# A cached-attention decode step with a gated MLP: output projections in column layout, the group tail deferred, eight K blocks prefetched

## The chip, the cores and the metric

The kernel runs on one core of a Trainium2 chip. The metric is device time in microseconds (us) of a whole execution; shorter is better. Six runs of the kernel before took between 417.31 and 419.82 us, with a median of 418.4 us.

## What is computed

One token goes through two branches whose results are mixed by a scalar gate. Branch A is attention with 32 query heads, 4 key/value heads and a cache of 65,536 positions. Branch B is a gated MLP on the same token. All tensors are bf16.

```
x = A_x                                        # (1, 1, 1024)
g = sigmoid((x * gate_w).sum(-1))
q = x @ wq                                     # 32 heads of 128
s = q @ k_cache^T * 128**-0.5                  # 4 KV heads, 8 query heads each, 65536 positions
a = (softmax(s) @ v_cache) @ wo                # wo: (4096, 1024)
z = gelu(x @ w_in)                             # w_in: (1024, 3584)
u = z[:1792] * (w_sp * layernorm(z[1792:]) + b_sp)
b = u @ w_out                                  # w_out: (1792, 1024)
out = g * a + (1 - g) * b                      # (1, 1, 1024)
```

K and V are 64 MiB each, the weights 26.5 MiB together; every byte is read once.

## The kernel before, in words

The kernel works in four **groups**, one for each KV head g. The cache of a group is cut into 16 K blocks and 16 V blocks of 4,096 positions (1 MiB each). Every large tile (K and V blocks, and all weight tiles) comes from one pool of 19 buffers of 8 KB per partition (`kv`, L83, `NKV = 19`), and all of these loads are issued on the queue of SP, in the order in which the program emits them. A scheduler in the framework settles the order on every engine, gives out buffers, and makes a load wait until its buffer is free. Each load also waits for the completion of the load eight places earlier, because there are eight semaphores for transfers; so eight are in flight at most.

**K blocks** (`k_block_work`, L290): a block has 32 chunks of 128 positions. PE transposes each chunk (`tps`, L296), eight to a PSUM tile; VectorE (DVE) or ScalarE (ACT) copies the tile to SBUF (`ktt`, L301 and L303); PE multiplies it with the eight query heads of the group (`spt`, L263). For every 64 chunks ACT casts the scores to `scT` (L271) and DVE takes a maximum over them (`mxp`, L275).

**stats** (L324), once per group after its last K block: the maximum over all positions goes through a transpose (`mxT`) and a matmul with ones (`nb_ps`) to `negm` on all partitions.

**The V phase**: in five parts, DVE adds `negm` to the scores (L444), ACT takes Exp (L448), DVE sums up (`Ssum`, L450), and PE accumulates 512 matmuls per group into one PSUM tile, `o_ps` (L456), 32 for each V block. There is one buffer for `o_ps`. Between V blocks the loop slips in other loads with their work: the two `wo` tiles of the group (`woa_t`), a few tiles of `w_in` with their `z` matmuls (L176), and the first `XK` K blocks of the next group. In the last group it slips in the four tiles of `w_out` (`wout_t`) instead.

**group_tail** (L342) ends each group: `l_ps` and its reciprocal, scaling of `o_ps` (`o_sc`, L351), a transpose to `oT` (L354, L355), and the product with this group's rows of `wo` (L365). Here the vector oT is the stationary operand (128 x 1) and `wo` the moving one (128 x 512), so that the result is one row of 1,024 on one partition, in two halves. DVE adds them to `a_acc` (L372, L374). `b_matmuls` (L237) makes `b_row` in the same way from `uT` and `w_out`. After the tail, the remaining K blocks of the next group follow, with the first `XV` = 3 V blocks among them.

**The end** (L479 to L484): two DVE instructions on one partition, `diff` and `orow`, mix a_acc, b_row and the gate, and one transfer writes the row. The gate itself is made at the start on one partition too, from `x_row` and `gw_row` (L113 to L118).

The loop over groups, before, in the lines that matter:

```
for g in range(G):
    flush_k(g)
    negm = stats(g)
    ...
    group_tail(g, o_ps, Ssum)
    if not last:
        rem = list(range(XK, NBLK))
        ...
```

Of the kernel before, what the change touches and what calls it, by code (L numbers as in the profile page):

```python
# [20 lines left out]
PST_BUFS = 3  # L21
LAG = 3
XV = 3
XK = 4


@with_exitstack
def kernel(
# [49 lines left out]
    win_groups = [min(i * (G - 1) // NWIN, G - 2) for i in range(NWIN)]  # L78

    const = ctx.enter_context(tc.tile_pool(name="const", bufs=1))  # L80
    rows = ctx.enter_context(tc.tile_pool(name="rows", bufs=1))
    wk = ctx.enter_context(tc.tile_pool(name="wk", bufs=2))
    kv = ctx.enter_context(tc.tile_pool(name="kv", bufs=NKV))  # L83
    ktp = ctx.enter_context(tc.tile_pool(name="ktp", bufs=KT_BUFS))
# [12 lines left out]

    x8 = const.tile([KC, P], BF16, name="x8")
    nc.scalar.dma_start(out=x8[:], in_=A_x.rearrange("o t (kc p) -> (o t kc) p", p=P))
    x_row = rows.tile([1, D], BF16, name="x_row")  # L100
    nc.scalar.dma_start(out=x_row[:], in_=A_x.rearrange("o t d -> (o t) d"))
    gw_row = rows.tile([1, D], BF16, name="gw_row")
    nc.scalar.dma_start(out=gw_row[:], in_=gate_w.rearrange("(o d) -> o d", o=1))
    wsp_b = const.tile([P, 1], BF16, name="wsp_b")
    nc.scalar.dma_start(out=wsp_b[:], in_=B_w_sp.rearrange("a b -> (a b)").to_broadcast((P, 1)))
    bsp_b = const.tile([P, 1], BF16, name="bsp_b")
# [3 lines left out]
    bsp_f = const.tile([P, 1], FP32, name="bsp_f")  # L110
    nc.vector.tensor_copy(out=bsp_f[:], in_=bsp_b[:])

    gprod = rows.tile([1, D], FP32, name="gprod")  # L113
    nc.vector.tensor_tensor(out=gprod[:], in0=x_row[:], in1=gw_row[:], op=ALU.mult)
    gsum = wk.tile([1, 1], FP32, name="gsum")
    nc.vector.reduce_sum(out=gsum[:], in_=gprod[:], axis=AX.X)
    gate = const.tile([1, 1], FP32, name="gate")
    nc.scalar.activation(out=gate[:], in_=gsum[:], func=ACT.Sigmoid)  # L118

    xT_ps = psm.tile([P, KC], BF16, name="xT_ps", tag="m")  # L120
    nc.tensor.transpose(xT_ps[:], x8[:], ident_b[:KC, :KC])  # L121
    xT = const.tile([P, KC], BF16, name="xT")
    nc.vector.tensor_copy(out=xT[:], in_=xT_ps[:])

    qacc = const.tile([P, H], FP32, name="qacc")
    for kc in range(KC):
# [96 lines left out]
                                scalar2=bsp_f[:, 0:1], op0=ALU.mult, op1=ALU.add)  # L223
        nc.vector.tensor_tensor(out=uT[:], in0=zg[:, 0:KC_OUT], in1=gb[:], op=ALU.mult)

    b_row = rows.tile([1, D], FP32, name="b_row")

    def b_matmuls():
        b_ps = [psm.tile([1, 512], FP32, name=f"b_ps{nb}", tag="m") for nb in range(NBH)]
        for i in range(NWOUT):  # L230
            ch0 = i * WO_CH
            ncks = min(WO_CH, KC_OUT - ch0)
            wo_t = wout_tiles[i]
            for kl in range(ncks):
                kcg = ch0 + kl
                for nb in range(NBH):
                    nc.tensor.matmul(  # L237
                        b_ps[nb][:, :], lhsT=uT[:, kcg:kcg + 1],
                        rhs=wo_t[:, kl, nb * 512:(nb + 1) * 512],
                        start=(kcg == 0), stop=(kcg == KC_OUT - 1),  # L240
                    )
        for nb in range(NBH):
            nc.vector.tensor_copy(out=b_row[:, nb * 512:(nb + 1) * 512], in_=b_ps[nb][:, :])  # L243

    oT = const.tile([P, H], BF16, name="oT")
    a_acc = rows.tile([1, D], FP32, name="a_acc")
    evac_i = [0]
    gs = [SimpleNamespace(scT=None, mxp=None, pending=[], spt=None, v_tiles={}) for _ in range(G)]

# [74 lines left out]
    def stats(g):  # L324
        st = gs[g]
        mx = wk.tile([P, REP], FP32, name="mx")
        nc.vector.tensor_reduce(out=mx[:], in_=st.mxp[:].rearrange("p b h -> p h b"),  # L327
                                axis=AX.X, op=ALU.max)
        mxT = psm.tile([REP, P], FP32, name="mxT", tag="m")
        nc.tensor.transpose(mxT[:], mx[:], ident_f[:])  # L330
        gm = wk.tile([REP, 1], FP32, name="gm")
        nc.vector.reduce_max(out=gm[:], in_=mxT[:], axis=AX.X)
        dg = wk.tile([REP, REP], FP32, name="dg")
        nc.vector.tensor_scalar(out=dg[:], in0=ident_f[:REP, :REP], scalar1=gm[:, 0:1],
                                scalar2=-1.0, op0=ALU.mult, op1=ALU.mult)
        nb_ps = psm.tile([P, REP], FP32, name="nb_ps", tag="m")
        nc.tensor.matmul(nb_ps[:], lhsT=ones_f[:REP, :], rhs=dg[:], start=True, stop=True)  # L337
        negm = wk.tile([P, REP], BF16, name="negm")
        nc.vector.tensor_copy(out=negm[:], in_=nb_ps[:])
        return negm  # L340

    def group_tail(g, o_ps, Ssum):  # L342
        ssum = wk.tile([P, REP], FP32, name="ssum")
        nc.vector.tensor_reduce(out=ssum[:], in_=Ssum[:].rearrange("p b h -> p h b"),
                                axis=AX.X, op=ALU.add)
        l_ps = psm.tile([REP, 1], FP32, name="l_ps", tag="m")
        nc.tensor.matmul(l_ps[:], lhsT=ssum[:], rhs=ones_f[:, 0:1], start=True, stop=True)
        rl = wk.tile([REP, 1], FP32, name="rl")
        nc.vector.reciprocal(out=rl[:], in_=l_ps[:])
        o_sc = wk.tile([REP, DH], BF16, name="o_sc")  # L350
        nc.vector.tensor_scalar(out=o_sc[:], in0=o_ps[:], scalar1=rl[:, 0:1], scalar2=None,  # L351
                                op0=ALU.mult)
        oT_ps = psm.tile([P, REP], BF16, name="oT_ps", tag="m")
        nc.tensor.transpose(oT_ps[:], o_sc[:], ident_b[:REP, :REP])  # L354
        nc.vector.tensor_copy(out=oT[:, g * REP:(g + 1) * REP], in_=oT_ps[:])  # L355
        a_ps = [psm.tile([1, 512], FP32, name=f"a_ps{nb}", tag="m") for nb in range(NBH)]
        for gi in range(WOA_PER_G):
            wi = g * WOA_PER_G + gi
            h0 = wi * WOA_CH
            woa = woa_tiles[wi]  # L360
            for hl in range(WOA_CH):
                h = h0 + hl
                hl_g = gi * WOA_CH + hl
                for nb in range(NBH):
                    nc.tensor.matmul(  # L365
                        a_ps[nb][:, :], lhsT=oT[:, h:h + 1],
                        rhs=woa[:, hl, nb * 512:(nb + 1) * 512],
                        start=(hl_g == 0), stop=(hl_g == REP - 1),
                    )
        for nb in range(NBH):  # L370
            if g == 0:
                nc.vector.tensor_copy(out=a_acc[:, nb * 512:(nb + 1) * 512], in_=a_ps[nb][:, :])  # L372
            else:
                nc.vector.tensor_tensor(out=a_acc[:, nb * 512:(nb + 1) * 512],  # L374
                                        in0=a_acc[:, nb * 512:(nb + 1) * 512],
                                        in1=a_ps[nb][:, :], op=ALU.add)

    def spread_positions(n, lo, hi):
        if n == 0:
# [7 lines left out]
    for blk in range(NBLK):  # L387
        kn = k_block_dma(0, blk)
        k_block_work(0, blk, kn)
        if blk in vpos0:  # L390
            v_block_dma(0, vb_next)
            vb_next += 1

    for g in range(G):
        flush_k(g)
        negm = stats(g)

        last = (g == G - 1)
        if not last:
# [63 lines left out]
            c0 += ceb  # L463
        assert not callbacks, callbacks.keys()

        group_tail(g, o_ps, Ssum)

        if not last:
            rem = list(range(XK, NBLK))
# [2 lines left out]
            for ri, blk in enumerate(rem):  # L472
                kn = k_block_dma(g + 1, blk)
                k_block_work(g + 1, blk, kn)
                if ri in vpos:
                    v_block_dma(g + 1, vb_next)
                    vb_next += 1

    diff = rows.tile([1, D], FP32, name="diff")  # L479
    nc.vector.tensor_tensor(out=diff[:], in0=a_acc[:], in1=b_row[:], op=ALU.subtract)  # L480
    orow = rows.tile([1, D], BF16, name="orow")
    nc.vector.scalar_tensor_tensor(out=orow[:], in0=diff[:], scalar=gate[:, 0:1], in1=b_row[:],
                                   op0=ALU.mult, op1=ALU.add)
    nc.sync.dma_start(out=out.rearrange("o t d -> (o t) d"), in_=orow[:])  # L484


# [28 lines left out]
```

## Time and profile before

| | |
|---|---|
| Median of six runs | 418.4 us |
| Profiled execution: whole time | 417.55 us |
| Profiled execution: span from the first instruction to the last | 415.8 us |
| PE (matmul) busy | 349.2 us (84%), 6,743 instructions |
| PE weight loads busy | 321.6 us (77%) |
| DVE busy | 209.3 us (50%), 325 instructions |
| ACT busy | 126.9 us (31%), 145 instructions |
| Read from HBM | 162.01 MB, 390 GB/s over the span |
| Granted clock of PE, mean | 0.963 |

The span is what the page and its views divide; the whole time has 1.75 us more around it. PE's matmuls are pipelined: one record of a matmul lasts longer than the distance to the next, so that a cost is taken from a row of many, as duration over count. The page's slices show the busy share of each engine in forty equal parts of the span (10.4 us each), in tenths; the row PEclk shows the clock that PE was granted, DMA the mean busy share of the sixteen DMA engines, and GB/s what they moved. A group takes about 92 us: four stretches of K work, stats and V work follow each other. The timeline has instructions in order of time: start, duration, engine, line, operation, result and operands, shapes and count, and in brackets how long the engine had been idle and what ended that.

### The profile page before, as it was taken

The numbers are of one execution on the slowest core, as the hardware profiler recorded it, in microseconds if no ns is written. First come the engines' busy times: TensorE is split into PE (matmuls) and PEld (weight loads), VectorE is DVE, ScalarE is ACT, GpSimd is POOL, SyncE is SP. The second block draws the span as 40 slices with busy tenths as digits, with TensorE's granted clock in tenths as the row PEclk, the third lists the DMA queues.
The fourth block names the chain that finished last, engine by engine and source line by source line (L and its number), as shares of the span: only waits on it lengthen the run. The fifth ranks groups of instructions, "written<-read, shape, count | busy, mean of one in ns | idle before, by whom it ended". The sixth has DMA issues, their size and how long they took to land.

```text
span 415.8 us, 14558 instructions
## 1 busy us (share of the span) xinstructions
PE 349.2 (84%) x6743; PEld 321.6 (77%) x6743; DVE 209.3 (50%) x325; ACT 126.9 (31%) x145; POOL 0.8 (0%) x7
## 2 busy tenths in 40 slices
PE   0548899789989999779999988859999998869993
PEld 0548888779988788779997777759999688868781
DVE  1224677792243486682142666675443576783014
ACT  1004454640031354431122444442231254550000
POOL 0000000000000000000000000000000000000000
PEclk9999999969999999969999999969999999969998
DMA  7999999999999999999999999999999999999930
GB/s 269 424 415 418 420 413 415 403 415 417 415 417 418 419 415 412 404 418 418 415 418 418 417 418 412 403 416 419 419 414 419 420 411 411 391 412 401 372 128 0
DMA packets 27186, 162.94 MB, mean 392 GB/s; under 512 B 2803, under 2 KB 2803, under 8 KB 9718
## 3 DMA queue, kind: packets, MB, share of 16 engines
q1 hardware_dynamic: 26818, 162.02, 95.4%
q8 instruction: 52, 0.85, 0.8%
q10 hardware_dynamic: 308, 0.01, 0.0%
q14 instruction: 8, 0.07, 0.0%
HBM read 162.01 MB, written 0.00 MB: 390 GB/s over the span
## 4 chain that ended last, share of the span: by engine, by line
PE 64%; ACT 13%; DVE 10%; DMA 6%; issue 6%; ACTq 1%; DVEq 0%
PE o_ps L456 30%; PE tps L296 19%; ACT ktt L301 10%; PE spt L263 7%; DVE ktt L303 6%; DMA kn<-in_A_k_cache_dram 4%; DMA bsp_b<-in_B_b_sp_dram 3%; ACT scT L271 2%; PE z_ps L176 2%; DVE mxp L275 1%; PE b_ps_8170 L237 1%; PE b_ps_8171 L237 1%; PE nb_ps L337 1%; PE a_ps_8245 L365 0%; PE a_ps_4644 L365 0%
## 5 line engine op out<-in xcount | busy, mean ns | idle before, releaser
L296 PE MATMUL tps<-ident_b,kn 128*128 128x128 bf16 x2048 | 138.4, 222 | 13.4 <-DVE ktt L303 7.8
L303 DVE COPY ktt<-tps 128x1024 bf16<-128x1024 bf16 x171 | 112.4, 686 | 70.4 <-PE tps L296 67.7
L301 ACT COPY ktt<-tps 128x1024 bf16<-128x1024 bf16 x85 | 86.0, 1012 | 181.9 <-PE tps L296 181.9
L296 PEld LDWEIGHTS <-kn 128*128 128x128 bf16 x2048 | 120.5, 99 | 19.0 <-issue 16.5
L456 PE MATMUL o_ps<-vt,scT 128*8 128x128 bf16 x2048 | 127.0, 226 | 4.1 <-ACT scT L448 4.1
L456 PEld LDWEIGHTS <-scT 128*8 128x8 bf16 x2048 | 121.5, 90 | 5.7 <-ACT scT L448 4.5
L263 PE MATMUL spt<-qT,ktt 128*128 128x8 bf16 x2048 | 76.8, 167 | 9.7 <-ACT ktt L301 4.5
L263 PEld LDWEIGHTS <-ktt 128*128 128x128 bf16 x2048 | 67.1, 96 | 15.2 <-ACT ktt L301 8.0
L275 DVE TENSOR_REDUCE mxp<-scT 128x8 f32<-128x512 bf16 x32 | 34.0, 1061 | 29.8 <-ACT scT L271 29.7
L450 DVE TENSOR_REDUCE Ssum<-scT 128x8 f32<-128x1024 bf16 (+2 forms) x20 | 31.0, 1596 | 2.4 <-ACT scT L448 2.4
L271 ACT CAST scT<-spt 128x512 bf16<-128x512 f32 x32 | 18.8, 588 | 19.0 <-PE spt L263 19.0
L448 ACT ACTIVATE scT<-scT 128x1024 bf16<-128x1024 bf16 (+2 forms) x20 | 16.7, 879 | 21.3 <-DVE scT L444 21.1
L131 PEld LDWEIGHTS <-wq_t 128*128 128x128 bf16 x256 | 7.2, 104 | 17.2 <-issue 13.0
L121 PE MATMUL xT_ps<-ident_b,x_94 8*128 8x8 bf16 x1 | 0.2, 161 | 15.0 <-DVE ident_b L94 15.0
L365 PEld LDWEIGHTS <-oT 128*1 128x1 bf16 x64 | 5.0, 84 | 8.7 <-DVE oT L355 1.4
L243 DVE COPY b_row<-b_ps_8170 1x512 f32<-1x512 f32 x1 | 0.7, 679 | 21.2 <-PE b_ps_8170 L237 21.2
L131 PE MATMUL q_ps<-xT,wq_t 128*128 128x1 bf16 x256 | 7.4, 165 | 4.3 <-DMA wq_t<-in_A_wq_dram 4.0
L183 DVE TENSOR_TENSOR zacc<-zacc,z_ps 128x28 f32<-128x28 f32 x7 | 1.3, 183 | 19.2 <-PE z_ps L176 19.2
L444 DVE TENSOR_TENSOR scT<-scT,negm 128x1024 bf16<-128x1024 bf16 (+2 forms) x20 | 10.6, 578 | 0.1
L330 PE MATMUL mxT<-ident_f,mx 128*8 128x128 f32 x4 | 1.4, 348 | 8.3 <-DVE mx L327 8.3
L351 DVE TENSOR_SCALAR o_sc<-o_ps,rl 8x128 bf16<-8x128 f32 x4 | 1.4, 339 | 12.8 <-PE o_ps L456 12.8
L330 PEld LDWEIGHTS mxT<-ident_f,mx 128*8 128x8 f32 x4 | 0.3, 83 | 8.7 <-DVE mx L327 6.5
(79 smaller groups left out, 87.2 us busy)
## 6 DMA issues: line engine op xcount, KB each, us to landing
kn<-in_A_k_cache_dram SPq DMA_DIRECT2D x64, 1024.0 KB, 19.9
vt<-in_A_v_cache_dram SPq DMA_DIRECT2D x64, 1024.0 KB, 19.9
wq_t<-in_A_wq_dram SPq DMA_DIRECT2D x8, 1024.0 KB, 10.6
woa_t<-in_A_wo_dram SPq DMA_DIRECT2D x8, 1024.0 KB, 20.1
wi_t<-in_B_w_in_dram SPq DMA_DIRECT2D x8, 896.0 KB, 18.5
wout_t<-in_B_w_out_dram SPq DMA_DIRECT2D x3, 1024.0 KB, 19.0
wout_t<-in_B_w_out_dram SPq DMA_DIRECT2D x1, 512.0 KB, 18.2
x_94<-in_A_x_dram ACTq DMA_DIRECT2D x1, 2.0 KB
```

Of the source, the lines that this page charges most:

```text
L131: nc.tensor.matmul(q_ps[:, h:h + 1], lhsT=wq_t[:, h * DH:(h + 1) * DH], rhs=xT[:, kc:kc + 1], start=True, stop=True,)
L176: nc.tensor.matmul(z_ps[:, mc:mc + 1], lhsT=wi_t[:, mc * P:(mc + 1) * P], rhs=xT[:, kc:kc + 1], start=True, stop=True,)
L263: nc.tensor.matmul(spt[:, (cg % CPS) * REP:(cg % CPS + 1) * REP], lhsT=lhs_getter(j), rhs=qT[:, g * REP:(g + 1) * REP], start=True, stop=True,
L271: nc.scalar.copy(out=st.scT[:, cb * CPS:(cb + 1) * CPS, :], in_=spt[:, :].rearrange("p (c h) -> p c h", h=REP),)
L275: nc.vector.tensor_reduce(out=st.mxp[:, cb, :], in_=st.scT[:, cb * CPS:(cb + 1) * CPS, :].rearrange("p c h -> p h c"), axis=AX.X, op=ALU.max,)
L296: nc.tensor.transpose(tps[:, j * P:(j + 1) * P], kn[:, c0 + j, :], ident_b[:])
L301: nc.scalar.copy(out=ktt[:], in_=tps[:])
L303: nc.vector.tensor_copy(out=ktt[:], in_=tps[:])
L444: nc.vector.tensor_tensor(out=scT[:, c0:c0 + ceb, :], in0=scT[:, c0:c0 + ceb, :], in1=negm[:].unsqueeze(1).to_broadcast([P, ceb, REP]), op ...
L448: nc.scalar.activation(out=PT[:, c0:c0 + ceb, :], in_=scT[:, c0:c0 + ceb, :], func=ACT.Exp, scale=SCALE)
L450: nc.vector.tensor_reduce(out=Ssum[:, eb, :], in_=PT[:, c0:c0 + ceb, :].rearrange("p c h -> p h c"), axis=AX.X, op=ALU.add,)
L456: nc.tensor.matmul(o_ps[:, :], lhsT=PT[:, cg, :], rhs=st.v_tiles[blk][:, c, :], start=(cg == 0), stop=(cg == NCG - 1),)
```

## The change

Five edits:

- **Column layout.** In `group_tail` and `b_matmuls` the weights are now the stationary operand (128 x 128) and the vector the moving one (128 x 1). The result is a tile of 128 partitions x 8 columns; column `nch` holds outputs 128 nch to 128 nch + 127. 16 matmuls of N = 512 per group become 64 of N = 1, and 28 become 112. The loop over output chunks is now the outer one, so that each column is accumulated to its end before the next begins. `a_acc`, `bT`, the differences and the mix are 128 x 8.
- **Output.** The 128 x 8 result is transposed on PE to 8 x 128 and written as eight rows.
- **Gate.** x and `gate_w` are loaded as 8 x 128, transposed, multiplied, summed per partition, and added up over partitions by a matmul with ones. The two row tiles and their pool go.
- **Deferred tail.** The tail of groups 0 to 2 is called after the `stats` of the next group; that of group 3 stays where it was.
- **XK = 8** in place of 4: eight K blocks of the next group come in the V phase, eight after it.

```diff
-XK = 4
+XK = 8
...
     def b_matmuls():
-        b_ps = [psm.tile([1, 512], FP32, name=f"b_ps{nb}", tag="m") for nb in range(NBH)]
...
+        b_ps = psm.tile([P, NCH_O], FP32, name="b_ps", tag="m")
+        for nch in range(NCH_O):
+            for kcg in range(KC_OUT):
+                i, kl = divmod(kcg, WO_CH)
+                wo_t = wout_tiles[i]
+                nc.tensor.matmul(
+                    b_ps[:, nch:nch + 1],
+                    lhsT=wo_t[:, kl, nch * P:(nch + 1) * P],
+                    rhs=uT[:, kcg:kcg + 1],
+                    start=(kcg == 0), stop=(kcg == KC_OUT - 1),
+                )
+        nc.vector.tensor_copy(out=bT[:], in_=b_ps[:])
...
+        a_ps = psm.tile([P, NCH_O], FP32, name="a_ps", tag="m")
+        for nch in range(NCH_O):
+            hl_g = 0
+            for gi in range(WOA_PER_G):
...
                     nc.tensor.matmul(
-                        a_ps[nb][:, :], lhsT=oT[:, h:h + 1],
-                        rhs=woa[:, hl, nb * 512:(nb + 1) * 512],
+                        a_ps[:, nch:nch + 1],
+                        lhsT=woa[:, hl, nch * P:(nch + 1) * P],
+                        rhs=oT[:, h:h + 1],
                         start=(hl_g == 0), stop=(hl_g == REP - 1),
                     )
...
+    deferred_tail = None
     for g in range(G):
         flush_k(g)
         negm = stats(g)
+        if deferred_tail is not None:
+            group_tail(*deferred_tail)
+            deferred_tail = None
...
-        group_tail(g, o_ps, Ssum)
+        if not last:
+            deferred_tail = (g, o_ps, Ssum)
+        else:
+            group_tail(g, o_ps, Ssum)
...
-    nc.vector.tensor_tensor(out=diff[:], in0=a_acc[:], in1=b_row[:], op=ALU.subtract)
...
-    nc.sync.dma_start(out=out.rearrange("o t d -> (o t) d"), in_=orow[:])
+    diffT = wk.tile([P, NCH_O], FP32, name="diffT")
+    nc.vector.tensor_tensor(out=diffT[:], in0=a_acc[:], in1=bT[:], op=ALU.subtract)
+    outT = wk.tile([P, NCH_O], BF16, name="outT")
+    nc.vector.scalar_tensor_tensor(out=outT[:], in0=diffT[:], scalar=gate[:, 0:1], in1=bT[:],
                                    op0=ALU.mult, op1=ALU.add)
+    o8_ps = psm.tile([NCH_O, P], BF16, name="o8_ps", tag="m")
+    nc.tensor.transpose(o8_ps[:], outT[:], ident_b[:])
+    o8 = wk.tile([NCH_O, P], BF16, name="o8")
+    nc.vector.tensor_copy(out=o8[:], in_=o8_ps[:])
+    nc.sync.dma_start(out=out.rearrange("o t (c p) -> (o t c) p", p=P), in_=o8[:])
```

## The prediction

> **What bounds the kernel now.** I read the slices of the page first, then the windows of the last 30 us, then the timeline of the tail.
>
> ```profile
> PEclk9999999969999999969999999969999999969998
> DMA  7999999999999999999999999999999999999930
> GB/s 269 424 415 418 420 413 415 403 415 417 415 417 418 419 415 412 404 418 418 415 418 418 417 418 412 403 416 419 419 414 419 420 411 411 391 412 401 372 128 0
> ```
>
> The transfers run at one rate (about 416 GB/s) from the second slice to the 38th. PE is 84% busy, but until the last stage it works in the shadow of the stream: 162 MB have to come in, and the change leaves every one of them. So only two things can move the end: when the last byte lands, and what follows it. The windows show the first.
>
> ```profile
> 390.00:392.00 2.00, 2.00 (x40) 2.00 (x38) 0.00 (x0) 0.00 (x0) 0.00 (x0) 1.00 1.03 416
> 394.00:396.00 2.00, 2.00 (x28) 1.59 (x27) 0.00 (x0) 0.00 (x0) 0.00 (x0) 1.00 0.57 232
> 402.00:404.00 2.00, 2.00 (x39) 2.00 (x37) 0.00 (x0) 0.00 (x0) 0.00 (x0) 1.00 0.03 12
> ```
>
> The last three columns are the granted clock, the DMA share and GB/s. From 392 on only half of the DMA engines still work, until 402. In the semaphore increments of the trace the slow half runs about 10 us behind the fast one: the last V block (issued at 384.1) lands between 392.86 and 402.89. A block is usable when the slowest engine is through, so for PE the stream ends at 402.9. The timeline has what comes then:
>
> ```profile
> 99.45 0.79 PE z_ps L176 x28
> ```
> ```profile
> 399.82 0.20 PE L347 MATMUL l_ps<-ones_f,ssum 128*8 128x1 f32 x2 [0.56 <-DVE b_row L243]
> 399.88 5.52 PE L456 MATMUL o_ps<-vt,scT 128*8 128x128 bf16 x96
> 405.44 0.34 DVE L351 TENSOR_SCALAR o_sc<-o_ps,rl 8x128 bf16<-8x128 f32 x1 [5.00 <-PE o_ps L456]
> 406.26 0.38 PE L365 MATMUL a_ps_8245<-woa_t,oT 128*1 128x512 bf16 x1 [0.25 <-DVE oT L355]
> 409.50 0.38 PE L365 MATMUL a_ps_8246<-woa_t,oT 128*1 128x512 bf16 x1
> 409.70 0.68 DVE L374 TENSOR_TENSOR a_acc<-a_acc,a_ps_8245 1x512 f32<-1x512 f32 x1 [3.49 <-PE a_ps_8245 L365]
> 411.00 1.21 DVE L480 TENSOR_TENSOR diff<-a_acc,b_row 1x1024 f32<-1x1024 f32 x1
> 412.25 1.27 DVE L482 SCALAR_TENSOR_TENSOR orow<-diff,gate,b_row 1x1024 bf16<-1x1024 f32 x1
> 413.55 0.32 SPq L484 DMA_DIRECT2D out_dram<-orow  x1
> ```
>
> The 96 matmuls are V blocks 13 to 15 of the last group without a pause, so block 15 starts at 399.88 + 64 x 0.0575 = 403.6, only 0.7 us after it landed: **PE and the stream end together**. Then come 8.1 us of serial tail (405.44 to 413.55), in which each vector instruction works on one partition, and 2.2 us for the output.
>
> **The change, part by part.**
>
> *Tail after the last o_ps.* o_sc and oT stay (0.82 us). The 16 matmuls of N = 512 take 409.70 - 406.26 = 3.44 us; 64 of N = 1 replace them. Price: L176 does 28 such (128x128 weights, one column) in 0.79 us, 28 ns each: 64 x 28 + 0.13 until DVE sees the last = 1.94. **-1.5**. The two a_acc additions, 411.00 - 409.70 = 1.30, become one of 128x8; the nearest row is zacc L183 (128x28, 183 ns), with its gap 0.21. **-1.1**. diff 1.25 and orow 1.30 become 0.21 each. **-2.1**. Added: a transpose of outT (like oT_ps: 0.05 + 0.22 until its reader starts) and a copy of 8x128 (at most o_sc's 0.34, plus 0.05). **+0.66**. The output goes out as eight rows of 256 B in place of one of 2 KB: x8 is read so and landed 1.39 us after its issue, the old output 1.16 us: 0 to +0.2, I take 0. Sum of the tail: **-4.0 us**.
>
> *b_matmuls.* 28 matmuls x 0.216 = 6.05 us on PE become 112 x 28 ns = 3.1; two 0.68 us copies, for which l_ps waited 0.56, become one small one. PE is 3.6 us earlier, but block 15 still has to land: it can start at 402.95 and not 403.6. **-0.6** in the best case; 0 at worst. Its place matters: the loop is now output chunk by chunk, so all but 12 of the 112 wait for the last wout transfer (landing 395.4). The built program's PE order is 224 o_ps, 4 b, 64 o_ps, 4 b, 64 o_ps, 4 b, 64 o_ps, 100 b, 96 o_ps. The 100 run from 396.0 to 398.8, and blocks 13 and 14 fit before 402.9.
>
> *Deferred group tail.* For groups 0 to 2 it moves behind the next group's stats. Today o_ps ends at 134.2 and the next transpose starts at 138.6: 4.4 us of PE time per group, of which the moved version keeps about 3 (l_ps to oT about 1, then 64 x 28 ns), in a place where PE waits 1 us for the first Exp anyway. It queues before the first o_ps of the next group, which waits for it, since there is one o_ps buffer. On DVE, rl, o_sc, oT and a_acc (0.15 + 0.34 + 0.16 + 0.2) go between the additions of L444. All of it is hidden by the stream. The price sits on SP: two woa tiles of the 19 buffers stay held through the next K phase, and in the built program two transfers per group wait for the a_ps matmuls of the tail. Cover: with eight transfers in flight each lands about 20 us after its issue.
>
> ```profile
> SPq L318 <- PE tps L296: 42.7, 21, 7.3
> 160.00:164.00 4.00, 3.87 (x90) 3.77 (x88) 2.49 (x4) 1.02 (x2) 0.00 (x0) 1.00 1.02 418
> ```
>
> SP has already stood for 7.3 us (160.7 to 168.0), and the DMA share stayed at 1.02. The new wait is about 5 us longer than the last K's release; 20 - 7.3 leaves some 12 us before it costs anything. I take 0; with the cover gone, its 5 us.
>
> *XK = 8.* Moves four K loads per group from the K phase to the V phase; the number of bytes before the last K block is the same. Today a pure K phase has 12 blocks at 3.05 us on PE (139.0 to 175.6), and PE falls behind: the last K block of group 3 landed at 354.1, its last score ended at 363.6. Now 8 blocks need 24.4 us while their 8 + 3 transfers take 27.5, so PE keeps up: last score about 358.3, first o_ps 4.7 us of stats and 3.4 of moved tail later, 366.5 against 368.3. From there 512 x 57.5 ns + 3.1 = 32.5 us, to 399.0 if nothing waited. That is before 402.9, so PE waits for the stream. Gain of its own: 0.
>
> *Start.* x_row and gw_row go, gw8 comes; two small transposes and a matmul with ones stand before the q matmuls, about 1 us later than 15.4. K block 0 lands at 28.3 whatever they do. DMA is slowed from 7 to 9 us by the two 2-byte broadcasts, and these stay. 0, within 0.3.
>
> *Clock gate.* Here a rule speaks against the change. The row first:
>
> ```profile
> 81.40:84.80 3.40, 0.65 (x3) 0.38 (x3) 1.81 (x4) 1.87 (x2) 0.00 (x0) 1.00 1.06 416
> 84.00:88.00 4.00, 2.56 (x23) 2.47 (x24) 3.45 (x9) 2.60 (x4) 0.00 (x0) 0.60 1.02 417
> ```
>
> After 3.4 us with little matmul work the clock is halved for 6.8 us (four times, once per stats). The Trainium skill ("TensorE: Matmul & The Clock Gate", the HAM clock gate) says that a free-running window of about 3.4 us decides, and that PE should have no idle gap over it. By the rule, the new wait of PE for V block 11 (block 10 done at 388.3, block 11 landing at 391.6: 3.3 us) fills no whole window: no loss. By the trace a window need not be empty (0.65 of 3.4 above), and N = 1 matmuls seem not to count: 4.7 us of q matmuls at 15.4 left the transposes at 28.3 at 3.61 us for 32, twice the warm time. Then the gap, or the 2.8 us of b matmuls, halves the clock in part of the phases. Half speed costs 1.6 us more per V block; 1 block at the end is 1.1 to 1.7, all three of the last 3.3. I take 0.4, between 0 and 3.3.
>
> **Sum** against the profiled execution: 415.8 - 4.0 - 0.6 + 0.4 = 411.6 us span; with its 1.75 us around the span (417.55), 413.3. The median shown is 418.4, 0.85 above that execution, so on that scale 418.4 - 4.2 = 414.2; I name **413.8**, between the two.
>
> **Rivals.**
>
> *N = 1 accumulation into one PSUM column is slow (ends slower than before).* L131 and L176 write each column once; now 8 or 14 matmuls in a row add to the same one. With x per matmul, the 100 b from 396.0, three blocks (5.5), the 0.85 to oT, 64 x, and 3.6 to the end give a span of about 406 + 164x: break-even at 60 ns, 419 (time 421) at 80 ns. Against it: l_ps above is two passes into one column in 0.20 us; with 166 ns for one, they are 34 ns apart. Chance 0.10.
>
> *The clock gate takes its whole price*: +3.3 instead of +0.4, 2.9 more than the forecast: 416.7. For it the two quiet stretches within 11 us of the end; against it that four V blocks lie between. Chance 0.10.
>
> *The stream's end moves.* The slow half of the engines falls back in steps of about 1.5 us in the semaphore increments; one step more through 560 more PE instructions to fetch, or a starved queue behind the held woa tiles, gives 415.3; a step less 412.3. Chance 0.12.
>
> *The projections are hidden anyway*: if the tail were beside other work, 418. The tail stands alone after 405.4, so 0.02.
>
> The forecast has 0.66. Range 411.8 to 416.8: it holds the forecast, both steps of the stream and half of the gate. About 0.5% (2.1 us) is what a measurement can tell: faster than 416.3 in the forecast, nearly all of the stream's case and a third of the gate's: 0.78; within 0.5% 0.12; slower 0.10.
>
> **What would show it.** Right: last V landing near 402.9 and o_ps ending near 405 with a wait for vt before blocks 11 and 15; the a_ps matmuls 28 ns apart; DVE pieces of 0.2 us; last issue near 409. Wrong: b or a_ps matmuls at 60 ns; a half clock after 390; the DMA share under 1 before 390; or a last score of group 3 still near 363.

## The result, and the profile after

| | before | after |
|---|---|---|
| Median | 417.79 us (20 runs, 416.85 to 419.92) | 413.73 us (10 runs, 412.08 to 417.18) |
| Ratio of the times | | 0.991, 95% interval 0.9881 to 0.9939 |
| Profiled execution, whole and span | 417.55 and 415.8 us | 413.78 and 411.9 us |
| PE busy, granted clock | 349.2 us, 0.963 | 348.6 us, 0.943 |

Six of the ten executions after took 412.1 to 413.9 us, at a granted clock of 0.943 to 0.956, the other four 415.6 to 417.2, at 0.939 to 0.944.

The forecast was 413.8. The number is met, but two of the steps that lead to it are not, and both show in the slices of the page after (clock in tenths, DMA share in tenths, GB/s; 40 slices of 10.3 us):

```profile
PEclk9999999969999999959998999959999999887998
DMA  7999999999999999999999999999999999999710
GB/s 276 423 422 426 423 422 425 414 426 425 425 423 422 426 422 421 419 425 424 425 422 426 425 425 418 417 427 426 422 427 422 426 422 410 421 411 399 317 49 2
```

The transfers run at some 424 GB/s and not at 416, although the same bytes are loaded. The last V block lands at 395.05 instead of 402.89 (last semaphore increment of the transfer). The windows near the end (columns as before: sum, PE, PE weight loads, DVE, ACT, POOL, clock, DMA share, GB/s) show what PE does meanwhile:

```profile
388.00:392.00 4.00, 4.00 (x75) 3.87 (x73) 0.00 (x0) 0.00 (x0) 0.00 (x0) 1.00 0.52 217
392.00:396.00 4.00, 4.00 (x74) 3.86 (x72) 0.00 (x0) 0.00 (x0) 0.00 (x0) 1.00 0.20 80
396.00:400.00 4.00, 4.00 (x121) 3.89 (x118) 0.00 (x0) 0.00 (x0) 0.00 (x0) 1.00 0.02 4
400.00:404.00 4.00, 4.00 (x85) 3.98 (x82) 0.17 (x1) 0.00 (x0) 0.00 (x0) 1.00 0.02 4
```

From 396 the DMA engines are quiet, and PE works on without a pause. It no longer ends together with the stream, it is 11 us behind it. So the stream got faster, and PE, which should have had time to spare, is late. The timeline has the end:

```profile
397.84 2.65 PE L238 MATMUL b_ps<-uT,wout_t 128*128 128x1 bf16 x100
400.42 5.52 PE L460 MATMUL o_ps<-vt,scT 128*8 128x128 bf16 x96
405.98 0.34 DVE L352 TENSOR_SCALAR o_sc<-o_ps,rl 8x128 bf16<-8x128 f32 x1 [5.29 <-PE o_ps L460]
406.80 1.74 PE L366 MATMUL a_ps<-oT,woa_t 128*128 128x1 bf16 x64 [0.25 <-DVE oT L356]
408.58 0.16 DVE L376 TENSOR_TENSOR a_acc<-a_acc,a_ps 128x8 f32<-128x8 f32 x1 [1.83 <-PE a_ps L366]
408.78 0.17 DVE L487 TENSOR_TENSOR diffT<-a_acc,bT 128x8 f32<-128x8 f32 x1
408.98 0.23 DVE L489 SCALAR_TENSOR_TENSOR outT<-diffT,gate,bT 128x8 bf16<-128x8 f32 x1
409.26 0.22 PE L492 MATMUL o_ps<-ident_b,outT 128*8 128x128 bf16 x1 [0.72 <-DVE outT L489]
409.52 0.21 DVE L494 COPY o_8538<-o_ps 8x128 bf16<-8x128 bf16 x1 [0.31 <-PE o_ps L492]
409.76 0.36 SPq L495 DMA_DIRECT2D out_dram<-o_8538  x1
```

From o_sc to the issue of the output it takes 409.76 - 405.98 = 3.78 us, before 413.55 - 405.44 = 8.11: 4.33 less. In the tail the column layout does what was forecast, and 100 matmuls of `b` take 2.65 us. The experiments have to say why the stream is faster, why PE is late, and what the deferred tail does.

### The profile page after: what moved, and what is told of

Its sections match the earlier page's. It is cut to its first block, busy times and chain, and to the rows that moved or that the text cites. A ratio compares the mean times of both kernels' runs of the same rounds, so it can differ in the third digit from the quotient of the medians.

```text
span 411.9 us, 15114 instructions
## 1 busy us (share of the span) xinstructions
PE 348.6 (85%) x7023; PEld 330.2 (80%) x7023; DVE 199.2 (48%) x322; ACT 127.7 (31%) x145; POOL 0.8 (0%) x7
## 4 chain that ended last, share of the span: by engine, by line
PE 62%; ACT 12%; DVE 11%; issue 7%; DMA 6%; ACTq 0%; DVEq 0%
PE o_ps L460 31%; PE tps L297 17%; ACT ktt L302 9%; DVE ktt L304 8%; PE spt L264 7%; DMA kn<-in_A_k_cache_dram 4%; ACT scT L272 3%; DMA bsp_b<-in_B_b_sp_dram 3%; PE a_ps L366 2%; PE z_ps L179 2%; DVE mxp L276 1%; PE b_ps L238 1%; PE nb_ps L338 1%; DVE scT L448 0%; PE mxT L331 0%
## 5 line engine op out<-in xcount | busy, mean ns | idle before, releaser
L297 PE MATMUL tps<-ident_b,kn 128*128 128x128 bf16 x2048 | 135.9, 222 | 15.2 <-DVE ktt L304 8.7
L460 PE MATMUL o_ps<-vt,scT 128*8 128x128 bf16 x2048 | 132.3, 229 | 1.1 <-ACT scT L452 1.0
L460 PEld LDWEIGHTS <-scT 128*8 128x8 bf16 x2048 | 124.1, 91 | 2.1 <-ACT scT L452 1.1
L264 PE MATMUL spt<-qT,ktt 128*128 128x8 bf16 x2048 | 77.2, 167 | 11.8 <-ACT ktt L302 5.1
L366 PEld LDWEIGHTS <-woa_t 128*128 128x128 bf16 x256 | 7.2, 102 | 1.0 <-issue 1.0
L366 PE MATMUL a_ps<-oT,woa_t 128*128 128x1 bf16 x256 | 7.3, 165 | 0.6 <-DVE oT L356 0.6
```

Source lines behind the costliest of these rows:

```text
L264: nc.tensor.matmul(spt[:, (cg % CPS) * REP:(cg % CPS + 1) * REP], lhsT=lhs_getter(j), rhs=qT[:, g * REP:(g + 1) * REP], start=True, stop=True,
L297: nc.tensor.transpose(tps[:, j * P:(j + 1) * P], kn[:, c0 + j, :], ident_b[:])
L366: nc.tensor.matmul(a_ps[:, nch:nch + 1], lhsT=woa[:, hl, nch * P:(nch + 1) * P], rhs=oT[:, h:h + 1], start=(hl_g == 0), stop=(hl_g == REP ...
L460: nc.tensor.matmul(o_ps[:, :], lhsT=PT[:, cg, :], rhs=st.v_tiles[blk][:, c, :], start=(cg == 0), stop=(cg == NCG - 1),)
```

## The experiments

Each kernel was timed beside the kernel before on the same chip (its median there: 419.12 in the first group of four, 418.37 in the second, 418.21 in the third); ratios are to that. The changed kernel was timed beside one of 417.79 us, so that its median stands 0.4 to 1.3 us low against the others; where the two differ, the ratio decides. Three theories for the first group: A, the gain is the shorter serial tail and the other edits are neutral; B, the gain comes from the prefetch or the deferred tail; C, the prefetch or the deferred tail costs time on PE.

### The edits apart

**Column layout alone** (gate and output edits included):

```diff
-XK = 8
+XK = 4
...
-        if not last:
-            deferred_tail = (g, o_ps, Ssum)
-        else:
-            group_tail(g, o_ps, Ssum)
+        group_tail(g, o_ps, Ssum)
```

> Column layout, output and gate edits alone; XK = 4 and the tail inline. Theory A (the gain is the serial tail, the other two edits are neutral): the stretch from o_sc to the output's issue is 3.8 us in place of 8.1, time 413.5 to 414. Theory B (XK = 8 or the deferral brought part of the gain): 415.5 or more. Theory C (XK = 8 and the deferral cost time, because PE runs at half clock longer and is late at the end): below 412.5, with four half-clock stretches of 6.8 us and block 15 of V waiting for its transfer or less than 2 us behind it.

Measured: 408.81 us (408.37 to 410.4), ratio 0.9767 (0.974 to 0.9794). This one edit brings more than the whole change. The time is in theory C's range, but not its marks: besides four half-clock stretches of 6.8 us there are three of 3.4, and block 15 of V starts some 5.6 us behind its transfer.

**Column layout and deferred tail, XK = 4** (of the changed kernel, only the constant):

```diff
-XK = 8
+XK = 4
```

> As the changed kernel, but XK = 4. Theory A: 413.5 to 414. Theory B: 415 or more if XK = 8 brought the gain. Theory C: 411.5 to 413 if XK = 8 is what slows PE; as the changed kernel (413.7) if it is the deferral, whose 64 matmuls of one column stand in the quiet stretch of stats and lengthen the half clock from 6.8 to 10.2 us.

Measured: 406.83 us (405.46 to 407.59), ratio 0.9708 (0.968 to 0.9736). It is faster than both kernels, and than any of the three theories had it.

**Column layout and XK = 8, tail in its old place:**

```diff
-        if not last:
-            deferred_tail = (g, o_ps, Ssum)
-        else:
-            group_tail(g, o_ps, Ssum)
+        group_tail(g, o_ps, Ssum)
```

> As the changed kernel, but the tail inline. Theory A: 413.5 to 414. Theory B: 415 or more if the deferral brought the gain. Theory C: 411.5 to 413 with half-clock stretches back at 6.8 us after each stats if the deferral slows PE; 413.7 if XK = 8 does.

Measured: 420.0 us (419.13 to 423.62), ratio 1.0043 (1.0019 to 1.0066). Theory B's 415 or more is met; theory C is missed in the kernel that was to show it.

**XK = 8 in the kernel before:**

```diff
-XK = 4
+XK = 8
```

> The kernel before with XK = 8 alone. Theory A: 417.8, within 0.5. Theory B: 416 or less. Theory C: 418.5 to 420, the last score of group 3 later than 363.6 against the landing of its K block.

Measured: 425.52 us (424.06 to 430.24), ratio 1.0181 (1.0132 to 1.023). The loss that theory C named, only larger.

What follows: the first half of theory C holds, for XK = 8. It costs 1.8% in the kernel before, 2.7% in the column layout with its tail in place (420.0 against 408.8) and, between 406.8 and 413.7 (0.9708 and 0.991), 7 to 8 us in the changed kernel. Theory B holds for the deferred tail: ratio 0.9708 against 0.9767, some 2 us, and at XK = 8 1.0043 against 0.991, some 6 us. Theory A as it stands falls as well: col_only gains 10 us, and the tail explains 4.3 of them. Its transfers, too, are faster: they land the last V block at 394.89.

### Where the load buffers lie

The change drops the pool `rows` and resizes two small pools. The pools are laid out one after another in SBUF, so that the 19 load buffers (8,192 bytes each) now start at byte 22,784 of each partition and not at 44,256. The first is a multiple of 64 (and of 256: 89 x 256), the second is 32 past one (224 past a multiple of 256). Theory P: this decides the rate of the stream. Theory Q: it does not. Two kernels swap the places, by an unused tile of 32 bytes that one memset writes. The tile moves the pools behind the load buffers (`scT` and `ktt`) by 32 bytes as well.

**The kernel before, buffers at 44,288 (a multiple of 64, and of 256):**

```diff
     nc.gpsimd.memset(ones_f[:], 1.0)
+    pad = const.tile([P, 8], FP32, name="pad")
+    nc.gpsimd.memset(pad[:], 0.0)
```

> The kernel before with one unused tile of 32 bytes per partition ahead of the pool of load buffers, so that these begin on a multiple of 64 bytes (44,288) and not 32 off (44,256). Theory P (the place of the load buffers sets the rate of the stream: 416 GB/s at 32 off, 424 on the multiple): 2.45 us per MB, last V landing near 395 in place of 402.9, time 412 to 416. Theory Q (the faster stream comes from the new layout or from the instructions it leaves out): as before, 417 to 419, last V near 403.

Measured: 416.56 us (415.31 to 417.4), ratio 0.9957 (0.9939 to 0.9974). The time is just above theory P's 412 to 416, the last V lands where P had it. Its row of the slices, one instruction and one tile away from the kernel before:

```profile
GB/s 266 429 424 425 425 423 421 418 424 424 424 425 425 424 425 421 418 425 422 426 425 425 424 425 416 421 425 425 428 422 425 425 419 408 415 422 420 212 2 0
```

**The version with XK = 4 and deferred tail, buffers at 22,816 (32 past a multiple):**

```diff
-XK = 8
+XK = 4
...
     nc.gpsimd.memset(ones_f[:], 1.0)
+    pad = const.tile([P, 8], FP32, name="pad")
+    nc.gpsimd.memset(pad[:], 0.0)
```

> Column layout and deferral at XK = 4 (406.8) with the same tile, which here moves the load buffers 32 bytes off the multiple of 64. Theory P: last V landing near 403 and at least 4 us more, 411 to 414. Theory Q: 406.8 within 1.

Measured: 413.94 us (412.87 to 415.84), ratio 0.9899 (0.987 to 0.9929). Its row:

```profile
GB/s 266 422 418 420 416 413 416 401 418 417 418 413 419 416 418 414 402 417 417 417 416 420 415 416 413 406 415 419 416 415 416 420 416 410 388 408 408 401 174 2
```

Theory P holds in both directions. Last landing of V: 394.84 and 403.09, against 402.89 and 395.12 without the pad. That it is the transfers themselves, and not `ktt` or a later issue, is in the queue's row of the pages (packets, MB, share of 16 engines' span), first the kernel before, then with the pad:

```profile
q1 hardware_dynamic: 26818, 162.02, 95.4%
q1 hardware_dynamic: 26818, 162.02, 93.8%
```

The same packets with the same bytes keep the DMA engines busy 1.8% less; one of 8,192 bytes takes 310.5 ns in the mean and not 316.5 (between 30 and 340 us), while DVE's ktt copies take 686 ns in both. The kernel before gains only 1.8 us from a stream that ends 8 us earlier, because PE was at its end as well; with XK = 4 and the column layout, PE is early and 7 to 8 us are lost when the stream is slow. At equal stream the column layout is worth 0.9767 against 0.9957, some 8 us. 4.3 of them are the tail. The rest, 3.4 us less PE work for `b`, 1.7 us less in each of the tails of groups 0 to 2, and on the other side half-clock stretches of 37.5 us in place of 27.3, was not timed apart.

**The changed kernel, buffers at 22,816:**

```diff
     nc.gpsimd.memset(ones_f[:], 1.0)
+    pad = const.tile([P, 8], FP32, name="pad")
+    nc.gpsimd.memset(pad[:], 0.0)
```

> The changed kernel with an unused tile of 32 bytes per partition ahead of the load buffers, so that they start at 22,816 as far from a multiple of 64 as those of the kernel before. Theory P with XK = 8's cost on PE: last V landing at 403.1 in place of 395.05, PE late by itself (last score 365 to 367), so the two ends meet again and the time is 415 to 419, close to the kernel before. Theory Q: 413.7 as the changed kernel. The forecast's own premise (stream to 402.9, PE keeps up) would give 413.8 here too, with the last score near 360.

Measured: 417.18 us (414.52 to 418.18), ratio 0.9961 (0.9941 to 0.998). Last V landing 402.95, last score of group 3 at 366.5. This is the change without the accident of the place, and its median is within 0.5% of the kernel before. With the stream of the forecast, the forecast would have been 3.4 us too low.

### What XK = 8 costs

All kernels with the fast stream land the last K block of group 3 between 347.4 and 348.0. What differs is how late PE is done with it (one profiled execution each):

| | last score, group 3 | first o_ps | half clock before the last o_ps | ratio |
|---|---|---|---|---|
| XK = 2 (col_defer_xk2) | 358.0 | 364.4 | 47.8 us | 0.972 |
| XK = 4 (col_defer) | 357.8 | 364.3 | 34.1 us | 0.9708 |
| XK = 6 (after_xk6) | 361.3 | 368.1 | 47.8 us | 0.9797 |
| XK = 8 (after) | 365.5 | 372.1 | 44.4 us | 0.991 |

The half-clock column does not follow the time: XK = 2 has most and is among the fastest. It also differs between executions of one kernel, whose mean granted clocks are 0.938 to 0.955 (XK = 2), 0.952 to 0.959 (XK = 4), 0.939 to 0.952 (XK = 6) and 0.939 to 0.956 (XK = 8). What counts is whether PE makes up for the loss before the end. With XK = 2 it waits for K blocks three more times after the first, until 145.8 us, so that what it lost before is hidden by the transfers. With XK = 4, 6 and 8 it waits for none after the first, at 28 us, and each loss of PE stays to the end.

Two of these rows are runs of their own. **XK = 2:**

```diff
-XK = 8
+XK = 2
```

> Column layout and deferral with XK = 2. Theory C (a K block that is worked off between V blocks and the coarser order it leaves make PE later, some 1.8 us per block and kernel): 403 to 406. If four was a best place between two losses: 408 or more.

Measured: 406.89 us (405.56 to 407.52), ratio 0.972 (0.9691 to 0.9749): no different from XK = 4, and neither of the two outcomes expected.

**XK = 6:**

```diff
-XK = 8
+XK = 6
```

> The changed kernel with XK = 6. The built order has 40 runs of 32 transposes (34 at XK = 4, 44 at XK = 8). Theory O by that count: about 60% of the 7 us between XK = 4 and XK = 8, so 409 to 412. Theory S: in proportion to the moved blocks, 410. Neither if it stays at 407 or jumps to 414: then the cost comes from a threshold, not from a count.

Measured: 410.15 us (407.84 to 411.99), ratio 0.9797 (0.9766 to 0.9828). The price is flat up to four blocks and then about 1% for every two. It agrees with both theories and separates none.

What PE waits for, as the groups of the changed kernel show it (busy time, mean, then idle time ahead of the group):

```profile
L297 PE MATMUL tps<-ident_b,kn 128*128 128x128 bf16 x2048 | 135.9, 222 | 15.2 <-DVE ktt L304 8.7 <-ACT ktt L302 4.9 <-DMA kn<-in_A_k_cache_dram 1.4
L460 PE MATMUL o_ps<-vt,scT 128*8 128x128 bf16 x2048 | 132.3, 229 | 1.1 <-ACT scT L452 1.0
L264 PE MATMUL spt<-qT,ktt 128*128 128x8 bf16 x2048 | 77.2, 167 | 11.8 <-ACT ktt L302 5.1 <-DVE ktt L304 3.9
```

The same with XK = 4:

```profile
L297 PE MATMUL tps<-ident_b,kn 128*128 128x128 bf16 x2048 | 136.1, 222 | 13.3 <-DVE ktt L304 7.3 <-ACT ktt L302 4.3 <-DMA kn<-in_A_k_cache_dram 1.4
L460 PE MATMUL o_ps<-vt,scT 128*8 128x128 bf16 x2048 | 130.0, 228 | 1.3 <-ACT scT L452 1.0 <-issue 0.3
L264 PE MATMUL spt<-qT,ktt 128*128 128x8 bf16 x2048 | 76.0, 167 | 10.4 <-ACT ktt L302 4.6 <-DVE ktt L304 2.9
```

The idle time ahead of transposes and scores is 15.2 + 11.8 = 27.0 us against 23.7: **+3.3 us, all of it waits for ktt copies; those for a K transfer are 1.4 us in both**. The rest is busy time: PE 348.6 us against 343.8 for the same instructions, and the half-clock stretches are 10 us longer. The two make 8.1 us; the spans differ by 7.1, the medians by 6.9. This is an account and no proof: the busy time is that of records with modelled ends, and how much of the 4.8 us is the clock's is not shown.

One place of such a wait, in the kernel before with XK = 8 (timeline, PE alone):

```profile
354.23 1.50 PE L296 MATMUL tps<-ident_b,kn 128*128 128x128 bf16 x24
356.73 0.61 PE L296 MATMUL tps<-ident_b,kn 128*128 128x128 bf16 x8 [1.00 <-DVE ktt L303]
357.18 0.74 PE L263 MATMUL spt<-qT,ktt 128*128 128x8 bf16 x24
358.12 0.35 PE L263 MATMUL spt<-qT,ktt 128*128 128x8 bf16 x8 [0.20 <-DVE ktt L303]
358.34 3.44 PE L296 MATMUL tps<-ident_b,kn 128*128 128x128 bf16 x32
```

24 transposes fill the three `tps` buffers, and the next eight wait 1 us for one of them; the block at 358.34 falls into a half-clock stretch (3.44 us for 32). That suggested theory O: the scheduler's order, 32 transposes in one go, is what costs; the built program has 44 such runs with XK = 8, 40 with XK = 6, 34 with XK = 4 and 28 with XK = 2. Theory S: the sharing of the V phase itself. With LAG = 2, scores come a chunk earlier, and no run is longer than 24.

**LAG = 2 in the changed kernel:**

```diff
-LAG = 3
+LAG = 2
```

> The changed kernel with LAG = 2 in place of 3 (scores follow their transposes two chunks later, not three). In the built PE order no 32 transposes stand in one go any more (44 such runs in the changed kernel, 24 at most here, then 8 scores, then the last 8 transposes). Theory O (what XK = 8 costs is PE standing at the fourth chunk of such a run, which needs one of three tps buffers back): PE's waits for ktt copies fall by several us, the last score of group 3 ends near 359 to 362 and the kernel takes 407 to 410. Theory S (the cost is the sharing itself: eight K blocks beside V blocks, copies late whatever the order): last score near 365 and 412 to 415. If a score that follows its copy by only two chunks has to wait for it, the time rises over 415.

Measured: 427.83 us (426.72 to 430.99), ratio 1.0236 (1.0205 to 1.0266). The view of PE's waits (total us, times, longest):

```profile
PE spt L264 <- DVE ktt L304: 18.0, 41, 1.0
PE spt L264 <- ACT ktt L302: 13.2, 39, 0.8
```

**LAG = 2 with XK = 4:**

```diff
-LAG = 3
+LAG = 2
...
-XK = 8
+XK = 4
```

> LAG = 2 on the version with XK = 4 (406.8 before, 34 runs of 32 transposes). Theory O: fewer waits here too, but the stream ends at 395.1 and the last group's V phase is bound by PE, so 403 to 406. Theory S: 406 to 408, no change that counts.

Measured: 412.51 us (411.39 to 412.77), ratio 0.9854 (0.983 to 0.9878).

Theory O falls in this form. The waits of the transposes go, but the scores now wait 31 us for the copies (9.0 us, 5.1 + 3.9, in the changed kernel). For XK = 8 the third outcome that the expectation named came true; for XK = 4 neither theory had 412.5. What the two runs show is that PE's pace in the K work hangs on the copies of DVE and ACT, and that the order decides how much of them is covered. XK = 8 costs more at LAG = 2 as well (427.8 against 412.5). **Open stays** why the waits grow when more than four K blocks stand beside V blocks; theory S, whose 412 to 415 for LAG = 2 was missed as well, is not shown either. What makes the half-clock stretches can be read from the traces, below.

### The clock

**32 unread transposes of the identity ahead of `mxT` in each stats, and 8 behind it, with XK = 4 and deferred tail.** They add work and no result, and are to keep PE from being quiet there. Theory G: the half clock after stats still delays the end.

```diff
-XK = 8
+XK = 4
...
+        warm = pst.tile([P, TG * P], BF16, name="tps")
+        for j in range(32):
+            nc.tensor.transpose(warm[:, (j % TG) * P:(j % TG + 1) * P], ident_b[:], ident_b[:])
         nc.tensor.transpose(mxT[:], mx[:], ident_f[:])
+        for j in range(8):
+            nc.tensor.transpose(warm[:, j * P:(j + 1) * P], ident_b[:], ident_b[:])
```

> Column layout and deferral at XK = 4, with 40 transposes of the identity that nobody reads put into the wait of stats, so that PE is not quiet there. Theory G (the half clock after every stats delays the end): no half-clock stretch after stats, first o_ps to last o_ps of the last group 3 us shorter, 402 to 405. If the half clock is hidden under the stream: 406.5 to 408.

Measured: 405.95 us (404.81 to 406.04), ratio 0.9697 (0.9666 to 0.9727), the lowest of all. Half clock falls from 34.1 to 27.3 us, and o_ps from 130.0 to 127.2 us busy. The gain over XK = 4 without it (0.9708, 0.968 to 0.9736) lies inside the intervals: a direction, not a proof. Nor does the edit do all that it was made for: the half clock after stats is gone in the first group only and lasts 6.8, 3.4 and 6.8 us in the others. And PE now catches up with the stream (3.0 us of waits for K blocks in place of 1.4, the last at 141.0), so that part of its gain could not show.

**What the clock follows.** In all 14 traces the changes of clock on record lie a whole number of 3.413 us apart. Cut each trace at these places and count in each window the columns that PE's matmuls moved: 128 for a transpose or a V matmul, 8 for a score, 512 and 1 for the old and the new form of `a_ps` and `b_ps`. Of 1,374 windows at full clock, the 99 that a half clock followed held 3,200 columns at most, the others 2,898 at least. Of 165 windows at half clock, the 89 that ended it held 3,008 at least, the others 2,944 at most. A limit of 3,000 columns puts 1,533 of the 1,539 right; V matmuls alone, at 57.5 ns each, put some 7,600 into a window. In the piece of timeline above, the window before the half clock at 358.52 has 20 transposes and 32 scores, 20 x 128 + 32 x 8 = 2,816: the wait of 1.0 us was enough. So a wait for ktt costs PE twice when it falls badly in a window, and which windows it falls into differs from one execution to the next. This was read from the traces afterwards; no run was made to test it.

## Why the prediction was right

The total was right because **two errors of opposite sign cancelled**, beside a core that was right. With column layout and deferred tail in all four, the runs fill a square:

| | stream slow, as forecast (last V near 403) | stream fast (near 395) |
|---|---|---|
| XK = 4 | 413.94 us (0.9899) | 406.83 us (0.9708) |
| XK = 8 | 417.18 us (0.9961) | 413.73 us (0.991) |

The forecast's premises, a slow stream and a PE that keeps up, are nearest to the upper left, and its 413.8 is met there. From there the faster stream takes off 7.1 us and XK = 8 adds 6.9; the other way round, XK = 8 adds 3.2 and the stream takes off 3.5 (by the ratios 8.0 and 8.5, or 2.6 and 2.1). Either way it is luck that they cancel: the two have nothing to do with each other, and neither was in the forecast.

- **Tail, -4.0 us: right.** Measured -4.33. The 64 matmuls took 1.74 us (1.94 expected), 27 ns each; DVE's small pieces 0.16 to 0.23; transpose and copy together 0.5 until the issue, 0.66 expected.
- **b_matmuls: right in duration, wrong in worth.** 100 took 2.65 us, 26.5 ns each, where 112 were put at 3.1. The -0.6, put so low because "block 15 still has to land", fell with the landing: with the faster stream PE never waits in the last V phase (windows above), so that its whole saving, some 3.4 us, should count. No run has `b` alone. The rival of slow accumulation into one column is refuted by the same row, its break-even being 60 ns.
- **The stream, "last V landing near 402.9": wrong**, 395.05. The number of bytes was counted, but not where they go: the edits to the small tiles moved the load buffers by an odd multiple of 32 bytes. Of the Trainium skill, "DMA: Bandwidth & Descriptors" (How a descriptor splits into AXI transactions) has what comes nearest: a descriptor is split into pieces of 256 bytes from boundaries of 256. By that page, and if its account of reads holds for writes too, a row of 8,192 bytes off a boundary takes 33 pieces and not 32, an estimate of 3%, and one of 2,048 bytes 9 and not 8, 12%. Measured are 1.9% (316.5 against 310.5 ns) and 3.4% (87.4 against 84.5 ns). The direction agrees, the sizes do not, so that the reason stays open. The rival "the stream's end moves" had steps of 1.5 us and other causes; it does not count as foreseen.
- **XK = 8, "so PE keeps up" and "Gain of its own: 0": wrong**, by 3.2 us with the slow stream of the forecast and 6.9 with the fast one. It was worked out that eight blocks at 3.05 us fit into the time of their transfers, with the last score at 358.3. It ended at 365.5. The sum took 3.05 us per block from a phase of twelve blocks and let the four moved blocks cost nothing extra in the V phase. In the changed kernel the last eight K blocks took 27.8 us (337.7 to 365.5) and not 24.4, and in the kernel before with XK = 8 27.5. 358 is where the version with XK = 4 ends (357.8).
- **The stream's shadow.** The text let PE work "in the shadow of the stream" until the last stage, and so hid all that the edits do to PE in groups 0 to 2. But in the kernel before PE waits for a K block once, for the first of all, and for a V block never:

```profile
PE tps L296 <- DMA kn<-in_A_k_cache_dram: 1.5, 1, 1.5
```

It was mostly 1 to 7 us behind its K blocks (start of the transposes against the landing), and with the stream 8 us faster (before_pad) it needs 416.56 us by itself. The shadow was as long as the slow stream, and no longer.

- **Deferred tail, 0: too low.** It gains some 2 us with XK = 4 and some 6 with XK = 8. The text saw the place where PE "waits 1 us for the first Exp anyway" and yet gave nothing for it, since the stream would hide it. PE's waits for Exp fall from 4.1 us to 1.0, three groups by 1 us. At XK = 8 the deferral also takes away three half-clock stretches of 3.4 us that follow the row of 64 one-column matmuls at its old place (147.8, 246.8 and 345.8 us); half clock falls from 64.9 to 44.4 us. The held buffers on SP did no harm: the last landing is the same with and without the deferral (395.12 and 394.89).
- **Clock gate, +0.4 at the end of the last group: right that it can happen, and luck that it did not.** In the changed kernel there is no half-clock stretch from 375.3 to the last o_ps: PE does not wait for V blocks there, and its row of `b` falls across the end of a window (399.2). In five of the eleven traces with the column layout that row lay within one, or all but a few of it, and the clock was halved for 3.4 us after it, as the prediction had allowed. But before 375 the changed kernel has 44.4 us at half clock against 27.3, spread over the groups, and as PE sets the end, they count where PE has matmuls to do. The prediction looked at the clock only near the end.

Where PE does wait for V blocks, in the version with XK = 4 and the slow stream, its windows show what the prediction had weighed:

```profile
387.00:391.00 4.00, 1.97 (x35) 1.78 (x33) 0.00 (x0) 0.00 (x0) 0.00 (x0) 0.96 1.00 411
391.00:395.00 4.00, 3.17 (x31) 3.17 (x31) 0.00 (x0) 0.00 (x0) 0.00 (x0) 0.50 0.78 317
...
398.00:401.00 3.00, 3.00 (x109) 2.87 (x107) 0.10 (x1) 0.00 (x0) 0.00 (x0) 0.99 0.47 186
401.00:405.00 4.00, 4.00 (x47) 4.00 (x44) 0.06 (x1) 0.00 (x0) 0.00 (x0) 0.58 0.12 45
```

PE works half of the first window (two waits, 0.62 and 2.25 us) and the clock is halved from 390.7 for 6.8 us. In the third it is busy throughout, but 2.65 us of it are the 100 one-column matmuls, and the clock is halved again from 401.0 for 3.4 us. The windows of 3.413 us before the two changes hold 22 V matmuls and 4 of one column (2,820 columns) and 13 V matmuls and 100 of one column (1,764). So the prediction's reading of the row was right ("a window need not be empty", and one-column matmuls "seem not to count"), and the rule of the Trainium skill ("TensorE: Matmul & The Clock Gate", the HAM clock gate), as the prediction had read it, no loss without an idle gap over some 3.4 us, is too mild here: the longest wait was 2.25 us.

What would have shown it wrong was named: "a last score of group 3 still near 363". It came, at 365.5, while the time agreed.

The better kernel is the change with XK = 4, 406.83 us: ratio 0.9708 where the change has 0.991.

## What to carry to other kernels

When an edit drops or adds a pool, look where the large load buffers start afterwards: here 32 bytes were 8 us of the stream, worth 1.8 us where PE was late as well and some 7 where it was not. Work that moves between phases under a transfer stream is free only as long as its engine's own lag against the stream stays covered; take the lag (last landing against last use) from the trace, see whether PE ever waits for a transfer, and price the moved work at the pace of the mixed phase. And judge a forecast by its marks in between, not by its total.

## What the runs showed of the hardware

- **Place of the load buffers.** With the buffers on a multiple of 64 bytes the transfers run at about 424 GB/s (a packet of 8,192 bytes takes 310.5 ns); 32 bytes past one, at about 416 (316.2 to 316.5 ns). The last V lands at 394.8 to 395.4 in the first kind (but for LAG = 2 with XK = 8, 398.5, whose last V load was issued only at 391.95) and at 402.9 to 403.3 in the second: before, before with XK = 8, and the two shifted kernels. Three pairs differ in the pad alone. The slow places were 224 and 32 bytes past a multiple of 256, the fast ones multiples of it, and the two slow ones cost the same; an offset of 64 or 128 was not tried, so that the runs do not tell 64 from 256.
- **Matmuls of one column.** With a 128x128 weight load each, accumulating 8 or 14 times into one PSUM column, they take 26.5 to 27.2 ns each, no more than those that write each column once (28 ns).
- **The clock follows the columns that PE moves.** It changes only at steps of 3.413 us, and goes to half, or back, by whether the window before held fewer or more than about 3,000 moving columns (1,533 of 1,539 windows). One-column matmuls add next to nothing, whether or not PE is busy with them. With the column layout and the tail in place, XK = 8 stretches the half clock from 37.5 to 64.9 us, in 12 pieces over the whole run, with the same instructions: short waits between runs of transposes and scores are enough.
